# w_sp transposed by the DMA crossbar from DRAM to SBUF in place of TensorE transposes and VectorE copies, and GELU in four instructions in place of one

## The chip, the cores and the metric

The kernel runs on one core of one Trainium2 chip. The metric is the device time of one execution in microseconds (us). Before the change the median of three runs is 1141.48 us (1138.74 to 1142.0).

## What is computed

One transformer block in bfloat16 on a sequence of T = 2048 tokens of width D = 1024: a segmented attention (32 heads of 32, four segments of 512 tokens, with a memory carried from segment to segment) and, behind it, a gated MLP that mixes tokens (gMLP). The change is in the second half. Cut to what matters there:

```python
def _B_ref(x, w_in, w_sp, b_sp, w_out):            # x: layernorm of h, [1, 2048, 1024]
    Fh = w_in.shape[-1] // 2                        # 1792
    z = gelu_tanh(x @ w_in)                         # [1, 2048, 3584]
    z1 = z[..., :Fh]
    z2 = layernorm(z[..., Fh:])
    g = einsum('ts,bsf->btf', w_sp, z2) + b_sp[None, :, None]
    return (z1 * g) @ w_out
h  = x + attention(layernorm(x))
h2 = h + _B_ref(layernorm(h), w_in, w_sp, b_sp, w_out)
```

`gelu_tanh(v)` is 0.5 v (1 + tanh(0.79788 (v + 0.044715 v^3))). The sum over s with w_sp needs w_sp with s on the partitions, and w_sp lies in DRAM with t along the rows: it has to be transposed.

## The kernel before

The kernel is written instruction by instruction. `_Plan.op` (L45) appends an instruction to the list of one engine with its semaphore waits; `_Plan.dma` (L72) does it for a transfer, on the queue of SyncE (SP) or GpSimd (POOL). Each engine works its list off in the order in which the Python code appended it, so the order of the code is the order on every engine. PSUM banks are handed out in rotation by `get_misc` (L278), eight of them in the second half of the kernel.

First comes the attention (`quad`, `seg_end`, L477 and L641), which writes h to the output tensor in DRAM. Then:

- Loading and normalising h. `hn1` (L741) loads 128 tokens of h, computes the layernorm (`ln_stats`, L320: bn_stats, bn_aggr, an addition on VectorE, a power on GpSimd at L328, two more on VectorE), and `hn2` (L752) transposes the result on TensorE (L339) and copies it out of PSUM on VectorE (L760). The 16 chunks are done four for each segment of 512 tokens; those of segment s+1 are spread as extra units between the blocks of segment s.
- The w_in stage, `C1_seg` (L787), once for each of the four segments. It has 30 blocks of eight matmuls (`proj8`, L383): 14 z1 blocks (features on the partitions, 512 tokens wide) and 16 z2 blocks (128 tokens on the partitions; for each of the four groups of tokens three blocks of 512 and one of 256 features). The order is z2 group, four z1, z2 group, four z1, z2 group, three z1, z2 group, three z1. Each block is closed by one ScalarE instruction (L818), which takes GELU of the PSUM bank into `Z1T` or `Z2G` and frees the bank. After the fourth z2 block of a group `z2_ln` (L779) runs the layernorm of `Z2G` into `Z2` on VectorE and GpSimd. One extra unit (hn1 or hn2) is taken after each z2 group and after each z1 block of odd number. The weights w_in lie whole in SBUF.
- The w_sp and w_out stage, `C2C3_block` (L887), for four blocks of 512 tokens. First 14 blocks of 16 matmuls with w_sp transposed (L902), each closed by two VectorE instructions (L905 adds b_sp, L908 multiplies by z1) into `YT`; then eight blocks of 14 matmuls with w_out (L929), closed by a VectorE addition of h (L933) and a store. Before the first, SP loads b_sp (L891); before each pair of the latter, SP loads h again (L920).
- w_sp transposed, `wsp_units` (L855): for each 128 rows of w_sp one load of 512 KB into one of two buffers (`WSPCH`), 16 TensorE transposes in two banks (L876), and two VectorE copies into `WSPT[bblk % 2]` (L879). The four units of block 0 stand between the w_in stage and the first w_sp matmul; those of block b+1 are put after the 2nd, 5th, 8th and 11th of the 14 blocks of block b. The first of them and the load of w_out (on POOL's queue, L845) wait until the w_in stage is over on TensorE, VectorE and ScalarE, since their buffers lie in the memory of w_in.

Of the kernel before, what the change touches and what calls it, by code (L numbers as in the profile page):

```python
# [5 lines left out]
BF16 = mybir.dt.bfloat16  # L6
# [5 lines left out]
T = 2048  # L12
# [4 lines left out]
L = 512  # L17
# [4 lines left out]
SCALE = DH ** (-0.5)  # L22
LN_EPS = 1e-5
MEM_EPS = 1e-6
NJ = [512, 384, 256, 128]
OFFJ = [0, 512, 896, 1152]
ESLOT = 1280
# [78 lines left out]
def bass_sequential_preLN__memory_aug_infini_attn__mixer_gmlp__prompt_kernel(  # L106
# [42 lines left out]
    d_x = [mksig("d_x0", True), mksig("d_x1", True)]  # L149
    d_xr = [mksig("d_xr0", True), mksig("d_xr1", True)]  # L150
    d_hr = [mksig("d_hr0", True), mksig("d_hr1", True)]
    d_wsp = [mksig("d_wsp0", True), mksig("d_wsp1", True)]
    d_brow = [mksig("d_brow0", True), mksig("d_brow1", True)]
    d_out = [mksig("d_out0", True), mksig("d_out1", True)]

# [11 lines left out]
    def tens(name, shape, dt, off):  # L167
        sz = int(np.prod(shape[1:])) * mybir.dt.size(dt)
        assert off % 32 == 0, (name, off)
        assert off + sz <= ARENA, (name, off, sz)  # L170
        return nc.alloc_sbuf_tensor_at(name, list(shape), dt, offset=abase + off)
# [68 lines left out]
    R_CTMP = R_WQKV + 57344  # L240
    HR = [tens("hr%d" % i, [128, D], BF16, R_CTMP + i * 2048) for i in range(2)]
    HN = [tens("hn0", [128, D], BF16, R_CTMP + 4096), tens("hn1", [128, D], BF16, R_XN2)]
    R_CT2 = R_HCH + 3072
    Z2G = tens("z2g", [128, FH], BF16, R_CT2)
    WOUT = tens("w_out", [128, 14, D], BF16, R_WQKV)
    WSPT = [tens("wspT0", [128, NTC, L], BF16, R_WQKV + 28672), tens("wspT1", [128, NTC, L], BF16, R_WQKV + 45056)]
    WSPCH = [tens("wspch0", [128, T], BF16, R_WQKV + 61440), None]
    YT = tens("yT", [128, 14, L], BF16, R_WO)
    FIN2 = [tens("fin2_%d" % i, [128, L], BF16, R_WO + 14336 + i * 1024) for i in range(2)]
    TMPG = tens("tmpg", [128, L], F32, R_CT2)  # L250
    BROW = [tens("brow0", [128, L], BF16, R_CT2 + 2048)]
    HR2 = [tens("hr2_0", [128, D], BF16, R_CT2 + 3072)]
    WSPCH[1] = tens("wspch1", [128, T], BF16, R_CT2 + 5120)

    PS = nc.alloc_psum_tensor("ps", [128, 8, 512], F32)

    def bank_f32(b):
        return PS[:, b, :]
# [507 lines left out]
    def hn_chunk(tc):  # L766
        hn1(tc)
        return hn2(tc)

    z2g_res = _Res()  # L770

    hnt_ready = {}
    for (kind, tc) in (("h1", 0), ("h1", 1), ("h2", 0), ("h1", 2), ("h2", 1), ("h1", 3), ("h2", 2), ("h2", 3)):
# [3 lines left out]
            hnt_ready[tc] = hn2(tc)  # L777

    def z2_ln(tc, t4):  # L779
        t = ln_stats(Z2G, 4, LN_EPS, [t4], csz=448)  # L780
        tz = P("dve", lambda e, tc=tc: e.tensor_scalar(Z2[:, tc, :], Z2G[:], SM4[:, 1:2], SM4[:, 2:3],
                                                      ALU.mult, ALU.add),
               waits=[t], sig=g_dve_pe)
        z2g_res.free = (g_dve_pe, tz[1])
        chain["ln"] = tz

    def C1_seg(s, extra_units):  # L787
        sbk = s % 2
        xu = list(extra_units)
        wready = [hnt_ready[4 * s + i] for i in range(4)] + [_w16(t_win)]  # L790
        z1blocks = []
        for fc in range(14):
            z1blocks.append(dict(kind="z1", fc=fc, ncols=512,
                                 lhs=(lambda i, fc=fc: WIN_LO[:, i, fc * 128:(fc + 1) * 128]),
                                 rhs=(lambda i: HNT[sbk][:, i, :]),
                                 out=Z1T[:, fc, s * 512:(s + 1) * 512], accum=None))
        z2blocks = []
        for tcl in range(4):
            tc = 4 * s + tcl
            grp = []  # L800
            for fb in range(4):
                w = 512 if fb < 3 else 256
                f0 = fb * 512
                grp.append(dict(kind="z2", tc=tc, tcl=tcl, fb=fb, ncols=w,
                                lhs=(lambda i, tcl=tcl: HNT[sbk][:, i, tcl * 128:(tcl + 1) * 128]),
                                rhs=(lambda i, f0=f0, w=w: WIN_HI[:, i, f0:f0 + w]),
                                out=Z2G[:, fb * 512:fb * 512 + w], accum=None))
            z2blocks.append(grp)
        blocks = z2blocks[0] + z1blocks[0:4] + z2blocks[1] + z1blocks[4:8] + z2blocks[2] + z1blocks[8:11] + \
            z2blocks[3] + z1blocks[11:14]  # L810
        for n, blk in enumerate(blocks):
            mb = get_misc()
            ncols = blk["ncols"]
            dst = bank_f32(mb)[:, 0:ncols]
            w = [misc[mb].free] + (wready if n == 0 else [])
            tp = proj8(blk["lhs"], blk["rhs"], dst, w, g_pe_act)
            wz = [z2g_res.free] if (blk["kind"] == "z2" and blk["fb"] == 0) else []
            t4 = P("act", (lambda e, dst=dst, o=blk["out"]: e.activation(o, dst, ACTF.Gelu_apprx_tanh)),  # L818
                   waits=[tp] + wz, sig=g_act_dve)
            misc[mb].free = t4  # L820
            if blk["kind"] == "z2" and blk["fb"] == 3:
                z2_ln(blk["tc"], t4)
                if xu:
                    xu.pop(0)()
            if blk["kind"] == "z1" and blk["fc"] % 2 == 1 and xu:
                xu.pop(0)()
        while xu:
            xu.pop(0)()
# [20 lines left out]
    yt_res = _Res()  # L849
    fin_res = [_Res(), _Res()]  # L850

    wsp_ctr = [0]
    wspch_res = [_Res(), _Res()]

    def wsp_units(bblk, first_waits):  # L855
        wb = WSPT[bblk % 2]
        wspt_res[bblk % 2].ready = []

        def unit(tcl):
            tc = 4 * bblk + tcl  # L860
            k = wsp_ctr[0] % 2
            wsp_ctr[0] += 1
            ch = WSPCH[k]
            tl = plan.dma("sp", ch[:], B_w_sp[tc * 128:(tc + 1) * 128, :], d_wsp[k],
                          waits=[wspch_res[k].free] + (list(first_waits) if tcl == 0 else []))
            for half in range(2):
                mb = get_misc()
                bb = bank_bf16(mb)
                w = [misc[mb].free, _w16(tl)]
                if tcl == 0 and half == 0:  # L870
                    w.append(wspt_res[bblk % 2].free)
                    w += list(first_waits)
                tok = None
                for kk in range(8):
                    sc = half * 8 + kk
                    tok = P("pe", (lambda e, kk=kk, sc=sc, bb=bb, ch=ch: e.transpose(  # L876
                        bb[:, kk * 128:(kk + 1) * 128], ch[:, sc * 128:(sc + 1) * 128], IDENT[:])),
                            waits=(w if kk == 0 else []), sig=(g_pe_dve if kk == 7 else None))
                te = P("dve", (lambda e, half=half, bb=bb, tcl=tcl: e.tensor_copy(  # L879
                    wb[:, half * 8:(half + 1) * 8, tcl * 128:(tcl + 1) * 128],  # L880
                    bb.rearrange("p (c n) -> p c n", c=8))), waits=[tok], sig=g_dve_pe)
                misc[mb].free = te
                wspt_res[bblk % 2].ready.append(te)
            wspch_res[k].free = (g_pe_dve, tok[1])
        return [lambda tcl=tcl: unit(tcl) for tcl in range(4)]

    def C2C3_block(bblk, extra_units):  # L887
# [29 lines left out]
        for tcl in range(4):  # L917
            tc = 4 * bblk + tcl
            b = 0
            thr = plan.dma("sp", HR2[b][:], out2d[tc * 128:(tc + 1) * 128, :], d_hr[b],  # L920
                           waits=[hr_res[b].free, t_pe_all_C1, t_dve_all_C1, t_act_all_C1])
            ftoks = []
            for half in range(2):
                mb = get_misc()
                dst = bank_f32(MISC[mb])
                w = [misc[mb].free, ylast, _w16(t_wout)]
                tok = None
                for fc in range(14):
                    tok = P("pe", (lambda e, fc=fc, half=half, tcl=tcl, dst=dst: e.matmul(  # L929
                        dst, YT[:, fc, tcl * 128:(tcl + 1) * 128], WOUT[:, fc, half * 512:(half + 1) * 512],  # L930
                        start=(fc == 0), stop=(fc == 13))),
                            waits=(w if fc == 0 else []), sig=(g_pe_dve if fc == 13 else None))
                tf = P("dve", (lambda e, half=half, dst=dst, b=b: e.tensor_tensor(  # L933
                    FIN2[half][:], dst, HR2[b][:, half * 512:(half + 1) * 512], ALU.add)),
                       waits=[tok, _w16(thr), fin_res[half].free], sig=g_dve_sp)
                misc[mb].free = tf
                ftoks.append(tf)
                to = plan.dma("sp", out2d[tc * 128:(tc + 1) * 128, half * 512:(half + 1) * 512], FIN2[half][:],
                              d_out[half], waits=[tf])
                fin_res[half].free = _w16(to)  # L940
            hr_res[b].free = ftoks[-1]
# [71 lines left out]
```

The softmax here doesn't subtract the row's maximum and nothing guards it: scores larger than these inputs give would overflow.

## Time and profile before

| what | value |
|---|---|
| median of three runs | 1141.48 us |
| the profiled execution's own time | 1142.0 us |
| its span (first to last instruction) | 1140.2 us |
| mean granted TensorE clock | 0.904 of full speed |
| TensorE matmuls busy | 947.2 us (83% of the span) |
| VectorE busy | 527.8 us (46%) |
| ScalarE busy | 304.3 us (27%) |
| GpSimd busy | 35.2 us (3%) |
| data moved by DMA | 54.53 MB, 48 GB/s in the mean |

All times in the profile are microseconds from the start of the span unless ns is said. L12 is line 12 of the kernel. PE is TensorE's matmuls (a transpose is one too), PEld its weight loads, DVE VectorE, ACT ScalarE, POOL GpSimd, SP SyncE. A row of the groups reads: line, engine, operation, output <- input, shapes, count, then busy us and mean ns of one, then the engine's idle time just before such instructions and what ended it. A row of the timeline reads: start, length, engine, line, operation, count, and in brackets idle time before it and what ended that. Matmuls are pipelined and their lengths are modelled, so what counts for them is the distance from start to start.

The stages by the timeline: the w_in stage runs from 600.3 us to the end of the last GELU at 806.2; the first matmul with w_sp starts at 825.5; the last store is issued at 1138.0.

### The profile page before, as it was taken

The numbers are of one execution on the slowest core, as the hardware profiler recorded it, in microseconds if no ns is written. First come the engines' busy times: TensorE is split into PE (matmuls) and PEld (weight loads), VectorE is DVE, ScalarE is ACT, GpSimd is POOL, SyncE is SP. The second block draws the span as 40 slices with busy tenths as digits, with TensorE's granted clock in tenths as the row PEclk, the third lists the DMA queues.
The fourth block names the chain that finished last, engine by engine and source line by source line (L and its number), as shares of the span: only waits on it lengthen the run. The fifth ranks groups of instructions, "written<-read, shape, count | busy, mean of one in ns | idle before, by whom it ended". The sixth has DMA issues, their size and how long they took to land.

```text
span 1140.2 us, 16027 instructions
## 1 busy us (share of the span) xinstructions
PE 947.2 (83%) x6735; PEld 483.9 (42%) x6848; DVE 527.8 (46%) x1448; ACT 304.3 (27%) x383; POOL 35.2 (3%) x68
## 2 busy tenths in 40 slices
PE   2978886688775898566749999999599999999998
PEld 1444443444333443233324545444344444444443
DVE  4066333886447853366454553632344253343332
ACT  0356651366313652144202333333100000000000
POOL 2000000000000000000000000100000000000000
PEclk9988989798985999765678999999799999999999
DMA  8010002000020004400021000000610310301102
GB/s 324 26 29 1 1 1 83 29 1 1 1 93 20 1 1 163 169 1 1 19 92 29 19 19 19 20 1 1 238 53 1 92 61 13 112 29 37 42 1 65
DMA packets 23305, 54.53 MB, mean 48 GB/s; under 512 B 2369, under 2 KB 6977, under 8 KB 23233
## 3 DMA queue, kind: packets, MB, share of 16 engines
q1 hardware_dynamic: 19152, 34.10, 9.6%
q0 software_dynamic: 4080, 19.40, 4.5%
q8 instruction: 54, 0.88, 0.3%
q14 instruction: 19, 0.15, 0.0%
HBM read 45.10 MB, written 8.39 MB: 47 GB/s over the span
## 4 chain that ended last, share of the span: by engine, by line
PE 68%; DVE 15%; ACT 6%; DMA 4%; issue 4%; POOL 1%; SPq 0%; DVEq 0%; ACTq 0%; POOLq 0%
PE ps L386 33%; PE ps L902 17%; PE ps L929 8%; ACT eall L520 4%; PE ps L513 3%; DVE stats L323 3%; PE ps L506 2%; DMA wqkv<-in_A_wv_dram 2%; PE ps L551 2%; PE ps L876 1%; DVE ta L579 1%; DVE tm L581 1%; POOL sm_58 L328 1%; PE ps L556 1%; PE ps L339 1%
## 5 line engine op out<-in xcount | busy, mean ns | idle before, releaser
L520 ACT ACTIVATE eall<-ps 128x2048 bf16<-128x2048 f32 (+3 forms) x128 | 158.6, 1239 | 173.0 <-PE ps L513 172.4
L386 PE MATMUL ps<-xnT,wqkv 128*128 128x512 bf16 x489 | 118.6, 388 | 11.3 <-DVE msum L635 4.6
L929 PE MATMUL ps<-w_out,yT 128*128 128x512 bf16 x437 | 96.8, 379 | 6.9 <-DVE yT L908 6.4
L902 PE MATMUL ps<-wspT_113,z_106 128*128 128x512 bf16 x439 | 99.1, 386 | 1.7 <-DVE wspT_113 L879 1.3
L902 PE MATMUL ps<-wspT_114,z_106 128*128 128x512 bf16 x440 | 96.6, 379 | 0.4
L905 DVE TENSOR_TENSOR tmpg<-ps,brow_120 128x512 f32<-128x512 f32 x56 | 38.7, 692 | 118.4 <-PE ps L902 103.6
L386 PE MATMUL ps<-wo,oT 128*128 128x512 bf16 x248 | 63.9, 412 | 21.8 <-DVE oT L652 21.6
L323 DVE BATCH_NORM_STATS2 stats<-z2g 128x6 f32<-128x448 bf16 x64 | 35.3, 614 | 90.9 <-ACT z2g L818 90.9
L386 PEld LDWEIGHTS ps<-xnT,wqkv 128*128 128x128 bf16 x512 | 47.3, 99 | 62.4 <-DVE msum L635 5.8
L929 PEld LDWEIGHTS ps<-w_out,yT 128*128 128x128 bf16 x448 | 43.5, 98 | 60.2 <-DVE yT L908 8.2
L902 PEld LDWEIGHTS ps<-wspT_113,z_106 128*128 128x128 bf16 x448 | 44.0, 99 | 53.9 <-issue 3.6
L902 PEld LDWEIGHTS ps<-wspT_114,z_106 128*128 128x128 bf16 x448 | 43.7, 98 | 51.9
L818 ACT ACTIVATE z2g<-ps 128x512 bf16<-128x512 f32 x64 | 34.8, 544 | 111.4 <-PE ps L386 111.4
L386 PE MATMUL ps<-wqkv,xnT 128*128 128x512 bf16 x248 | 59.0, 391 | 4.5 <-DVE msum L635 3.6
L513 PE MATMUL ps<-negtri,ident 128*128 128x128 bf16 x512 | 61.6, 256 | 0.0
L506 PE MATMUL ps<-qT_70,kT_72 32*128 32x512 bf16 (+3 forms) x256 | 25.0, 380 | 33.6 <-ACT eall L520 33.6
L386 PE MATMUL ps<-w_in_hi,hnT_103 128*128 128x512 bf16 (+1 forms) x251 | 51.6, 364 | 1.4 <-DVE hnT_103 L760 1.2
L818 ACT ACTIVATE z1T<-ps 128x512 bf16<-128x512 f32 x56 | 33.4, 597 | 70.7 <-PE ps L386 70.7
L386 PE MATMUL ps<-hnT_104,w_in_lo 128*128 128x512 bf16 x217 | 49.4, 379 | 0.4
L386 PE MATMUL ps<-w_in_hi,hnT_104 128*128 128x512 bf16 (+1 forms) x253 | 49.6, 352 | 0.2
L386 PE MATMUL ps<-hnT_103,w_in_lo 128*128 128x512 bf16 x218 | 49.3, 379 | 0.3
L386 PEld LDWEIGHTS ps<-wo,oT 128*128 128x128 bf16 x256 | 25.6, 104 | 55.2 <-issue 13.4
(138 smaller groups left out, 1073.5 us busy)
## 6 DMA issues: line engine op xcount, KB each, us to landing
wspch_115<-in_B_w_sp_dram SPq DMA_DIRECT2D x8, 512.0 KB, 4.1
wspch_122<-in_B_w_sp_dram SPq DMA_DIRECT2D x8, 512.0 KB, 4.2
hr_0_121<-out_dram SPq DMA_DIRECT2D x16, 256.0 KB, 2.8
w_in_lo<-in_B_w_in_dram POOLq DMA_DIRECT2D x1, 3584.0 KB, 12.2
w_in_hi<-in_B_w_in_dram POOLq DMA_DIRECT2D x1, 3584.0 KB, 22.8
w_out<-in_B_w_out_dram POOLq DMA_DIRECT2D x1, 3584.0 KB, 17.8
xch_87<-in_A_x_dram SPq DMA_DIRECT2D x8, 256.0 KB, 2.8
xch_88<-in_A_x_dram SPq DMA_DIRECT2D x8, 256.0 KB, 3.0
```

The lines of the kernel that those rows point to most:

```text
L323: t = P("dve", (lambda e, ci=ci: e.bn_stats(STATS[:, ci, :], eng_in_ap[:, ci * csz:(ci + 1) * csz])), waits=((list(first_wait) + [chain["l ...
L328: tp = P("pool", lambda e: e.tensor_tensor(SM4[:, 1:2], SM4[:, 0:1], MHALF[:], ALU.pow), waits=[t], sig=g_pool)
L339: tok = P("pe", (lambda e, i=i: e.transpose(bb[:, i * 128:(i + 1) * 128], src_tile[:, col0 + i * 128: col0 + (i + 1) * 128], IDENT[:])), w ...
L386: tok = P("pe", (lambda e, i=i: e.matmul(dst, lhs_of_i(i), rhs_of_i(i), start=(i == 0), stop=(i == 7))), waits=(waits if i == 0 else []), ...
L506: P("pe", (lambda e, i=i, dst=dst: e.matmul(dst, kT[32 * i:32 * (i + 1), c, j * 128:(j + 1) * 128], qT[32 * i:32 * (i + 1), c, 128 * j:512 ...
L513: tp = P("pe", (lambda e, dstd=dstd: e.matmul(dstd, IDENT[:], NEGTRI[:], start=False, stop=True)), sig=(g_pe_act if i == 3 else None))
L520: ta = P("act", (lambda e: e.activation(dst4, src4, ACTF.Exp, scale=float(SCALE))), waits=wa, sig=g_act_pe)
L551: fn = (lambda e, i=i, j=j, h=h: e.matmul(dstb[:, i * 128:i * 128 + 33], ESALL[:, i, OFFJ[j] + (cq - j) * 128: OFFJ[j] + (cq - j + 1) * 12 ...
L818: t4 = P("act", (lambda e, dst=dst, o=blk["out"]: e.activation(o, dst, ACTF.Gelu_apprx_tanh)), waits=[tp] + wz, sig=g_act_dve)
L902: tok = P("pe", (lambda e, sc=sc, fc=fc, dst=dst: e.matmul(dst, Z2[:, sc, fc * 128:(fc + 1) * 128], wb[:, sc, :], start=(sc == 0), stop=(s ...
L905: t1 = P("dve", lambda e, dst=dst: e.tensor_tensor(TMPG[:], dst, BROW[0][:], ALU.add), waits=[tok, _w16(tb), tmpg_res.free], sig=g_dve_pe)
L929: tok = P("pe", (lambda e, fc=fc, half=half, tcl=tcl, dst=dst: e.matmul(dst, YT[:, fc, tcl * 128:(tcl + 1) * 128], WOUT[:, fc, half * 512: ...
```

## The change

Two things are done.

GELU of the w_in product, one ScalarE instruction before, is computed by four: ScalarE squares the PSUM bank (t1, Square) into `X2T`; VectorE forms (v^2 + 1/0.044715) v (t2, scalar_tensor_tensor, which reads the bank again) into `WG`; ScalarE takes Tanh of that, scaled (t3), into `TH`; VectorE forms (tanh + 1) v (t4, scalar_tensor_tensor, which reads the bank a third time and frees it) into `Z1T` or `Z2G`. t3 and t4 of a block are put after t1 and t2 of that block and ahead of t1 and t2 of the next one. The three small buffers are double. The result is twice GELU: the factor 2 falls out of the layernorm of z2 (whose eps is multiplied by 4), and for z1 it is taken out by a factor 0.5 in the last addition (L933 becomes scalar_tensor_tensor).

w_sp goes from DRAM to `WSPT` by one DMA with transposition for each 128 rows, on SP's queue, straight into the place that the VectorE copies wrote; the chunk buffers, the TensorE transposes and the copies are dropped. Each of the eight places (two buffers of four) has its own semaphore, and the w_sp matmuls wait for those of their block.

```diff
-            t4 = P("act", (lambda e, dst=dst, o=blk["out"]: e.activation(o, dst, ACTF.Gelu_apprx_tanh)),
-                   waits=[tp] + wz, sig=g_act_dve)
-            misc[mb].free = t4
...
+        for n in range(len(blocks) + 1):
+            blk = blocks[n] if n < len(blocks) else None
+            if prev is not None:
...
+                t3 = P("act", (lambda e, g=g, ncols=ncols: e.activation(TH[g][:, 0:ncols], WG[g][:, 0:ncols], ACTF.Tanh,
+                                                                    scale=float(GELU_C))),
+                       waits=[prev["t2"], th_res[g].free], sig=g_act_dve)
+                wg_res[g].free = t3
+                if prev["accum"] is None:
+                    t4 = P("dve", (lambda e, g=g, ncols=ncols, dst=dst, o=prev["out"]: e.scalar_tensor_tensor(
+                        o, TH[g][:, 0:ncols], 1.0, dst, ALU.add, ALU.mult)), waits=[t3], sig=g_dve_pe)
...
+                th_res[g].free = t4
+                misc[prev["mb"]].free = t4
+                if prev["kind"] == "z2" and prev["fb"] == 3:
+                    z2_ln(prev["tc"], t4)
+                    if xu:
+                        xu.pop(0)()
+            if blk is not None:
...
+                tp = proj8(blk["lhs"], blk["rhs"], dst, w, g_pe_act)
...
+                t1 = P("act", (lambda e, g=g, ncols=ncols, dst=dst: e.activation(X2T[g][:, 0:ncols], dst, ACTF.Square)),
+                       waits=[tp, x2t_res[g].free], sig=g_act_dve)
+                t2 = P("dve", (lambda e, g=g, ncols=ncols, dst=dst: e.scalar_tensor_tensor(
+                    WG[g][:, 0:ncols], X2T[g][:, 0:ncols], float(GELU_K), dst, ALU.add, ALU.mult)),
+                       waits=[t1, wg_res[g].free], sig=g_dve_act)
+                x2t_res[g].free = t2
+                blk["t2"] = t2
+            prev = blk
+            if blk is not None and blk["kind"] == "z1" and blk["fc"] % 2 == 1 and xu:
                 xu.pop(0)()
...
         def unit(tcl):
             tc = 4 * bblk + tcl
-            k = wsp_ctr[0] % 2
...
-            tl = plan.dma("sp", ch[:], B_w_sp[tc * 128:(tc + 1) * 128, :], d_wsp[k],
-                          waits=[wspch_res[k].free] + (list(first_waits) if tcl == 0 else []))
-            for half in range(2):
...
-                for kk in range(8):
-                    sc = half * 8 + kk
-                    tok = P("pe", (lambda e, kk=kk, sc=sc, bb=bb, ch=ch: e.transpose(
-                        bb[:, kk * 128:(kk + 1) * 128], ch[:, sc * 128:(sc + 1) * 128], IDENT[:])),
-                            waits=(w if kk == 0 else []), sig=(g_pe_dve if kk == 7 else None))
-                te = P("dve", (lambda e, half=half, bb=bb, tcl=tcl: e.tensor_copy(
-                    wb[:, half * 8:(half + 1) * 8, tcl * 128:(tcl + 1) * 128],
-                    bb.rearrange("p (c n) -> p c n", c=8))), waits=[tok], sig=g_dve_pe)
...
+            wfree = [wspt_res[bblk % 2].free] + list(first_waits) if tcl == 0 else []
+            tl = plan.dma("sp", wb[:, :, tcl * 128:(tcl + 1) * 128], B_w_sp[tc * 128:(tc + 1) * 128, :],
+                          d_wsp[4 * (bblk % 2) + tcl], waits=wfree, transpose=True)
+            wspt_res[bblk % 2].ready.append(_w16(tl))
...
-                tf = P("dve", (lambda e, half=half, dst=dst, b=b: e.tensor_tensor(
-                    FIN2[half][:], dst, HR2[b][:, half * 512:(half + 1) * 512], ALU.add)),
+                tf = P("dve", (lambda e, half=half, dst=dst, b=b: e.scalar_tensor_tensor(
+                    FIN2[half][:], dst, 0.5, HR2[b][:, half * 512:(half + 1) * 512],
+                    ALU.mult, ALU.add)),
```

Not shown: the constants `GELU_C` and `GELU_K`, the declarations of the buffers and semaphores, and 4 x eps in `z2_ln` (L780).

More of the change, by code (lines that the diff above doesn't have):

```diff
@@ L24 @@
 MEM_EPS = 1e-6
+GELU_C = 0.7978845608028654 * 0.044715
+GELU_K = 1.0 / 0.044715
 NJ = [512, 384, 256, 128]
@@ L151, in bass_sequential_preLN__memory_aug_infini_attn__mixer_gmlp__prompt_kernel @@
     d_hr = [mksig("d_hr0", True), mksig("d_hr1", True)]
-    d_wsp = [mksig("d_wsp0", True), mksig("d_wsp1", True)]
+    d_wsp = [mksig("d_wsp%d" % i, True) for i in range(8)]
     d_brow = [mksig("d_brow0", True), mksig("d_brow1", True)]
@@ L242, in bass_sequential_preLN__memory_aug_infini_attn__mixer_gmlp__prompt_kernel @@
     HN = [tens("hn0", [128, D], BF16, R_CTMP + 4096), tens("hn1", [128, D], BF16, R_XN2)]
+    X2T = [tens("x2t%d" % i, [128, L], BF16, R_CTMP + 6144 + i * 1024) for i in range(2)]
     R_CT2 = R_HCH + 3072
     Z2G = tens("z2g", [128, FH], BF16, R_CT2)
+    WG = [tens("wg%d" % i, [128, L], BF16, R_CT2 + 3584 + i * 1024) for i in range(2)]
+    TH = [tens("th%d" % i, [128, L], BF16, R_CT2 + 5632 + i * 1024) for i in range(2)]
     WOUT = tens("w_out", [128, 14, D], BF16, R_WQKV)
     WSPT = [tens("wspT0", [128, NTC, L], BF16, R_WQKV + 28672), tens("wspT1", [128, NTC, L], BF16, R_WQKV + 45056)]
-    WSPCH = [tens("wspch0", [128, T], BF16, R_WQKV + 61440), None]
     YT = tens("yT", [128, 14, L], BF16, R_WO)
@@ L252, in bass_sequential_preLN__memory_aug_infini_attn__mixer_gmlp__prompt_kernel @@
     HR2 = [tens("hr2_0", [128, D], BF16, R_CT2 + 3072)]
-    WSPCH[1] = tens("wspch1", [128, T], BF16, R_CT2 + 5120)
     PS = nc.alloc_psum_tensor("ps", [128, 8, 512], F32)
@@ L768, in hn_chunk @@
         return hn2(tc)
+    x2t_res = [_Res(), _Res()]
+    wg_res = [_Res(), _Res()]
+    th_res = [_Res(), _Res()]
     z2g_res = _Res()
+    gctr = [0]
+    t_z1_done = {}
     hnt_ready = {}
@@ L779, in z2_ln @@
     def z2_ln(tc, t4):
-        t = ln_stats(Z2G, 4, LN_EPS, [t4], csz=448)
+        t = ln_stats(Z2G, 4, 4.0 * LN_EPS, [t4], csz=448)
         tz = P("dve", lambda e, tc=tc: e.tensor_scalar(Z2[:, tc, :], Z2G[:], SM4[:, 1:2], SM4[:, 2:3],
@@ L810, in C1_seg @@
             z2blocks[3] + z1blocks[11:14]
[L811 to L818, printed above, removed]
-                   waits=[tp] + wz, sig=g_act_dve)
-            misc[mb].free = t4
[L821 to L825, printed above, removed]
+        prev = None
@@ new lines, in C1_seg @@
+        for n in range(len(blocks) + 1):
+            blk = blocks[n] if n < len(blocks) else None
+            if prev is not None:
+                g = prev["g"]
+                ncols = prev["ncols"]
+                dst = prev["dst"]
+                t3 = P("act", (lambda e, g=g, ncols=ncols: e.activation(TH[g][:, 0:ncols], WG[g][:, 0:ncols], ACTF.Tanh,
[5 more added lines that the diff above has]
+                        o, TH[g][:, 0:ncols], 1.0, dst, ALU.add, ALU.mult)), waits=[t3], sig=g_dve_pe)
+                else:
+                    t4 = P("dve", (lambda e, g=g, ncols=ncols, dst=dst, o=prev["out"], ac=prev["accum"]:
+                                  e.scalar_tensor_tensor(o, TH[g][:, 0:ncols], 1.0, dst, ALU.add, ALU.mult,
+                                                         accum_out=ac)), waits=[t3], sig=g_dve_pe)
+                th_res[g].free = t4
[5 more added lines that the diff above has]
+            if blk is not None:
+                g = gctr[0] % 2
+                gctr[0] += 1
+                blk["g"] = g
+                mb = get_misc()
+                blk["mb"] = mb
+                ncols = blk["ncols"]
+                dst = bank_f32(mb)[:, 0:ncols]
+                blk["dst"] = dst
+                w = [misc[mb].free] + (wready if n == 0 else [])
+                if blk["kind"] == "z2" and blk["fb"] == 0:
+                    w.append(z2g_res.free)
+                tp = proj8(blk["lhs"], blk["rhs"], dst, w, g_pe_act)
+                if blk["kind"] == "z1" and blk["fc"] == 13:
+                    t_z1_done[s] = tp
+                t1 = P("act", (lambda e, g=g, ncols=ncols, dst=dst: e.activation(X2T[g][:, 0:ncols], dst, ACTF.Square)),
[7 more added lines that the diff above has]
+            if blk is not None and blk["kind"] == "z1" and blk["fc"] % 2 == 1 and xu:
@@ L850, in bass_sequential_preLN__memory_aug_infini_attn__mixer_gmlp__prompt_kernel @@
     fin_res = [_Res(), _Res()]
-    wsp_ctr = [0]
-    wspch_res = [_Res(), _Res()]
     def wsp_units(bblk, first_waits):
@@ L860, in unit @@
             tc = 4 * bblk + tcl
-            k = wsp_ctr[0] % 2
-            wsp_ctr[0] += 1
-            ch = WSPCH[k]
-            tl = plan.dma("sp", ch[:], B_w_sp[tc * 128:(tc + 1) * 128, :], d_wsp[k],
-                          waits=[wspch_res[k].free] + (list(first_waits) if tcl == 0 else []))
-            for half in range(2):
[L867 to L873, printed above, removed]
-                for kk in range(8):
-                    sc = half * 8 + kk
-                    tok = P("pe", (lambda e, kk=kk, sc=sc, bb=bb, ch=ch: e.transpose(
-                        bb[:, kk * 128:(kk + 1) * 128], ch[:, sc * 128:(sc + 1) * 128], IDENT[:])),
-                            waits=(w if kk == 0 else []), sig=(g_pe_dve if kk == 7 else None))
-                te = P("dve", (lambda e, half=half, bb=bb, tcl=tcl: e.tensor_copy(
-                    wb[:, half * 8:(half + 1) * 8, tcl * 128:(tcl + 1) * 128],
-                    bb.rearrange("p (c n) -> p c n", c=8))), waits=[tok], sig=g_dve_pe)
-                misc[mb].free = te
-                wspt_res[bblk % 2].ready.append(te)
-            wspch_res[k].free = (g_pe_dve, tok[1])
+            wfree = [wspt_res[bblk % 2].free] + list(first_waits) if tcl == 0 else []
+            tl = plan.dma("sp", wb[:, :, tcl * 128:(tcl + 1) * 128], B_w_sp[tc * 128:(tc + 1) * 128, :],
+                          d_wsp[4 * (bblk % 2) + tcl], waits=wfree, transpose=True)
+            wspt_res[bblk % 2].ready.append(_w16(tl))
         return [lambda tcl=tcl: unit(tcl) for tcl in range(4)]
```

## The prediction

> **What bounds the kernel now.** I read the table of engines first (TensorE is busy 83% of the span, VectorE 46%, ScalarE 27%), then the chain that ended last, then the stages by time windows, and last the timeline of the stages that the change touches. The page's chain, in shares of the span:
>
> ```profile
> PE 68%; DVE 15%; ACT 6%; DMA 4%; issue 4%; POOL 1%; SPq 0%; DVEq 0%; ACTq 0%; POOLq 0%
> ```
>
> TensorE sets the end, but the share is a mean. The windows show the stages (columns: stretch, its length, busy us and count of PE, PEld, DVE, ACT, POOL, granted clock, DMA share, GB/s):
>
> ```profile
> 653.83:705.50 51.67, 50.28 (x269) 25.28 (x273) 25.84 (x60) 17.06 (x30) 4.40 (x8) 1.00 0.08 21
> 806.20:825.50 19.30, 7.31 (x64) 6.68 (x66) 5.54 (x8) 0.00 (x0) 1.12 (x1) 0.69 0.94 337
> 825.50:880.00 54.50, 54.19 (x283) 25.88 (x286) 22.85 (x35) 0.00 (x0) 0.00 (x0) 0.95 0.10 33
> ```
>
> The reader is to see three things. In the w_in stage (600.3 to 806.2 us; the first line is one of its four segments) TensorE is full at full clock, and GELU on ScalarE takes a third of the time, hidden. Between 806.2 and 825.5 TensorE is nearly idle and the DMA engines are 94% busy at 337 GB/s: first w_sp chunks and w_out together. In the w_sp stage (from 825.5) TensorE is full again.
>
> One block in the w_in stage, from the timeline (start, length, engine, line):
>
> ```profile
> 657.70 0.60 ACT L818 ACTIVATE z2g<-ps 128x512 bf16<-128x512 f32 x1 [1.13 <-PE ps L386]
> 659.42 0.60 ACT L818 ACTIVATE z2g<-ps 128x512 bf16<-128x512 f32 x1 [1.13 <-PE ps L386]
> 660.30 0.38 ACT L818 ACTIVATE z2g<-ps 128x256 bf16<-128x256 f32 x1 [0.28 <-PE ps L386]
> 660.71 2.21 DVE L323 BATCH_NORM_STATS2 stats<-z2g 128x6 f32<-128x448 bf16 x4 [6.94 <-ACT z2g L818]
> 662.96 0.26 DVE L325 BATCH_NORM_AGGREGATE mv<-stats 128x2 f32<-128x24 f32 x1
> 664.07 0.16 DVE L330 SCALAR_TENSOR_TENSOR sm_58<-mv,sm_58 128x1 f32<-128x1 f32 x1 [0.66 <-POOL sm_58 L328]
> 664.26 0.75 DVE L781 TENSOR_SCALAR z_106<-z2g,sm_58 128x1792 bf16<-128x1792 bf16 x1
> ```
>
> A 512-column block comes every 1.72 us (657.70 to 659.42), TensorE's eight matmuls. After each group of four z2 blocks VectorE runs a layernorm of 4.30 us (660.71 to 665.01), 0.66 of it waiting for GpSimd.
>
> **What the Trainium skill says.** "TensorE: Matmul & The Clock Gate", Architectural detail, says that ScalarE's and VectorE's queues are strict FIFO; the trace agrees (L330 and L781 wait behind GpSimd's 0.55 us step, and nothing of VectorE passes them). "ScalarE: Activation LUTs", Table sets, puts tanh in exp's set and says that cheap functions are filler in all sets; the trace has two table loads of 1283 ns in all and nothing on Square. "DMA: Bandwidth & Descriptors", Latency and other measured facts, has 261 GB/s for DMA transposes with a non-contiguous middle dimension; "VectorE: DVE Perf Modes", The three transpose paths, has 1309 ns for one 128x128 crossbar transpose. No row of the trace before shows a DMA transpose.
>
> **Part 1: GELU, of which the diff makes four instructions.** For each of 120 blocks the one L818 ACTIVATE (hidden) goes; Square and Tanh on ScalarE and two scalar_tensor_tensor on VectorE come. In program order ScalarE does tanh(n), square(n+1); VectorE does t4(n), then the layernorm if n ends a z2 group, then t2(n+1). tanh(n) needs t2(n), t4(n) needs tanh(n), and t2(n+1) stands behind t4(n). So t2, tanh, t4 of one block are in series with those of the next; two buffers do not loosen this. Prices:
>
> ```profile
> L406 DVE SCALAR_TENSOR_TENSOR pqT_74<-qe,pqT_74 128x512 bf16<-128x512 bf16 x16 | 11.1, 692 | 0.5
> L579 DVE TENSOR_TENSOR ta<-ps,rd 128x128 f32<-128x128 f32 x96 | 28.0, 291 | 3.3
> L302 ACT ACTIVATE g_53<-betab 128x32 f32<-128x32 bf16 x1 | 0.2, 229 | 1.8 <-DMA betab<-in_A_beta_dram 1.8
> 143.02 1.02 ACT L441 ACTIVATE tmpe<-ps 128x1024 bf16<-128x1024 bf16 x1 [0.31 <-DVE pk_66 L445]
> 144.07 0.69 DVE L442 TENSOR_SCALAR pk_66<-ps 128x1024 bf16<-128x1024 bf16 x1 [1.15 <-ACT tmpe L441]
> ```
>
> - t2 and t4 at 512 columns: 0.69 each (L406; L933, out of PSUM, has 692 too). At 256: between 291 at 128 and 692 at 512, 0.425.
> - tanh out of SBUF: L302 has 229 ns at 32 columns; L818's 384 and 597 ns at 256 and 512 give 0.833 ns a column; so 0.63 at 512 and 0.42 at 256, estimates.
> - hand-overs: ScalarE to VectorE 0.03 to 0.04 (144.04 to 144.07); VectorE to ScalarE 0.09 (L445 ended at 142.93, L441 began at 143.02).
> - a VectorE instruction whose data are there starts 0.08 before the end of the one ahead (four L323 of 0.61 take 2.21), so t4 to t2 is 0.61. square(n+1), 0.60, lies beside t4(n) and ends first.
>
> Period of a 512 block: 0.69 + 0.09 + 0.63 + 0.04 + 0.61 = 2.05 us against TensorE's 1.72. Of a 256 block: 0.425 + 0.09 + 0.42 + 0.04 + 0.345 = 1.32. Layernorm is no longer hidden: VectorE cannot start t2 before it ends. Sum:
> - 56 z1 blocks x 2.05 = 114.8.
> - 16 z2 groups x (3 x 2.05 + 1.32 + 4.30 + 0.03) = 188.8.
> - input layernorms of the next segment, 12 at 3.2 (two of them start at 613.64 and 616.87) and 12 copies of 0.66 (L760): 46. Where a unit stands after an odd z1 block, it fills the 0.75 in which VectorE waits for tanh; of 24 units 15 do, 9 of them copies of 0.66 and 6 of them layernorms worth 0.75: 10 off, 36 left.
>
> Together 339.6. The first GELU starts at 603.5 and its Square is over at 604.1, so the stage ends at 943.7 instead of 806.2: **+137.5**. TensorE, with eight banks to run ahead in, is off the path here. Of VectorE's own work in this stage nothing disappears. ScalarE has 240 x 0.6 = 144 us, not a bound. For bounds: if the tanh waits were covered entirely, VectorE alone would take 339.6 - 105 x 0.75 = 261, +59; if every hand-over and every wait were 0.1 us worse, 120 x 0.2 = +24 more.
>
> **Part 2: w_sp by the crossbar.** Removed in the w_sp stage: 12 chunks x 16 transposes, 1.06 us each time:
>
> ```profile
> 845.98 1.06 PE L876 MATMUL ps<-ident,wspch_122 128*128 128x128 bf16 x16
> ```
>
> TensorE is the bound there, so 12 x 1.06 = **-12.7**. The VectorE copies L879 (24 x 0.69) were hidden behind TensorE: nothing. Their replacement, SP's transposes for blocks 1 to 3, has a whole block (some 74 us) for 2.1 MB; cover is gone only below 2.1 MB / 74 us = 28 GB/s. They stand on SP's queue ahead of the hr load of L920, and block 0's ahead of the L891 load of b_sp; TensorE has eight PSUM banks for that delay (8 x 3.45 = 27 us of L902 work for b_sp, 8 x 3.02 = 24 of L929 work for hr); a load later than that would cost what goes beyond.
>
> The gap of 19.3 us before the first L902 matmul: four transposes of 512 KB instead of loads, transposes and copies, beside w_out (3.67 MB) on the same engines. From below: 2.1 MB and an equal share of w_out at the 337 GB/s of the window, 4.2/337 = 12.5, plus about 2 to land (a 256 KB load lands in 2.6): 14.5. At the page's 261 GB/s: 16 + 2 = 18. From above: 64 tiles x 1309 ns in series, 84. I take 20, slightly over the page's rate because the destination here is written in 256-byte pieces: **+0.7**, with -5 to +65 as ends.
>
> **Part 3: one-answer edits.** L933 becomes scalar_tensor_tensor: 692 ns before (L933) and after (L406), nothing. 4 x eps: nothing. A tanh table load is at most 1.3 us, in place of GELU's at 554.5: nothing.
>
> **Sum**, against the profiled execution's 1142.0 us (span 1140.2): 1142.0 + 137.5 - 12.7 + 0.7 = 1267.5. The median of three runs is 1141.48, 0.5 lower: 1267. Its own range, with hand-overs and the gap from 14.5 to 30: 1248 to 1292.
>
> **Rivals.**
> - A slow crossbar: at 84 us for four chunks the gap is +65, and each block of 74 us waits some 9 to 10 us more for its successor's chunks: +28 over three. 1267 + 65 + 28 = 1360. For it: the tile price, and that nothing before shows the operation. Against: the 261 GB/s. Half-way prices give 1300 to 1340. 25%.
> - TensorE falls to half clock in the layernorm pauses and becomes the bound: at the stage's start eight weight loads stand 0.43 apart instead of 0.21, so 104 x 3.42 + 16 x 1.71 = 383 instead of 339.6: 1310. Against: a pause lasts 4 to 8 us and eight full banks absorb a slow block or two. 5%.
> - Square and Tanh in different table sets: 240 loads x 1.283 = +308: 1575. Against: the page's filler rule. 3%.
> - Not slower: VectorE is overlapped after all. If t2 of the next block could pass t4 and the layernorm's wait, the stage would be bound by busy time alone; with some 100 us of present VectorE work and the 206 + 12.7 that may be spent, it decides at (218 - 100) / 240 = 0.49 us for each added instruction. At the cheapest pass of VectorE here (L746, 546 ns for 1024 columns; L781, 746 for 1792; so 0.41 for 512) the time would be 1142.0 - 12.7 + 0.7 = 1130. Against: 692 ns in every row with a second tensor operand, and the queue's order. 2%.
> - The chain runs shorter than worked out, by tanh waits that fall beside more of VectorE's work than I count: 1215 to 1248. 5%.
>
> The forecast has the remaining 60%. About 0.3% (3.4 us) is what a measurement of this kernel can tell from no change; slower has 0.98, faster and same 0.01 each. The range 1240 to 1350 takes in the forecast's own range, the upper part of the short chain, half clock and the half-way crossbar, leaving out about 2 in 10.
>
> **What would show it.** Right: C1 blocks spaced 2.05 us, VectorE idle 0.75 per block until tanh, TensorE idle for VectorE t4, the stage some 340 us; no L876; a gap of 15 to 25 us before L902. Wrong: Square rows with table loads between them; C1 matmuls 0.43 apart throughout; transposes landing later than 25 us, or L902 waiting for DMA in blocks 1 to 3.

## The result, and the profile after

| | before | changed |
|---|---|---|
| median | 1140.81 us (4 runs, 1138.74 to 1142.0) | 1258.99 us (4 runs, 1257.72 to 1260.2) |
| profiled execution: own time, span | 1142.0, 1140.2 us | 1259.37, 1257.6 us |
| ratio, 95% interval | | 1.1038 (1.1017 to 1.1059) |

The changed kernel is 118 us slower; 1267 was forecast. The two spans differ by 117.4 us, and the timelines say where:

| stretch | before | changed | difference |
|---|---|---|---|
| start to the first w_in matmul | 600.29 | 599.33 | -0.96 |
| w_in stage, to the end of the last GELU | 205.89 | 334.24 | +128.35 |
| gap to the first w_sp matmul | 19.32 | 21.99 | +2.67 |
| w_sp and w_out stage, to the end | 314.70 | 302.04 | -12.66 |

The chain of the changed kernel's page, in shares of the span:

```profile
PE 47%; DVE 30%; ACT 11%; issue 4%; DMA 3%; POOL 2%; SPq 2%; DVEq 0%; ACTq 0%; POOLq 0%
```

TensorE's share of the chain went from 68 to 47%, VectorE's from 15 to 30: the bound moved. Two windows of the changed kernel (length, busy us and count of PE, PEld, DVE, ACT, POOL, clock, DMA share, GB/s), the first inside the w_in stage, the second the gap:

```profile
640.00:692.00 52.00, 37.49 (x162) 17.05 (x167) 37.69 (x71) 20.48 (x39) 2.20 (x4) 0.82 0.04 11
933.63:955.50 21.87, 0.00 (x0) 0.00 (x0) 0.00 (x0) 0.00 (x0) 1.12 (x1) 0.50 0.97 268
```

In 52 us TensorE runs 162 recorded matmuls where it ran some 270 before, with VectorE at 72%. The gap is still full of DMA, at 268 GB/s where it was 337. VectorE and ScalarE in the w_in stage, from the timeline (start, length, engine, line; in brackets idle time ahead and what ended it; TensorE's rows are left out):

```profile
628.77 0.68 DVE L859 SCALAR_TENSOR_TENSOR wg_114<-x2t_111,ps 128x512 bf16<-128x512 bf16 x1
629.49 0.63 ACT L825 ACTIVATE th_116<-wg_114 128x512 bf16<-128x512 bf16 x1 [0.86 <-DVE wg_114 L859]
630.02 0.58 ACT L857 ACTIVATE x2t_112<-ps 128x512 bf16<-128x512 f32 x1
630.15 0.69 DVE L830 SCALAR_TENSOR_TENSOR z2g<-th_116,ps 128x512 bf16<-128x512 bf16 x1 [0.70 <-ACT th_116 L825]
630.75 0.68 DVE L859 SCALAR_TENSOR_TENSOR wg_115<-x2t_112,ps 128x512 bf16<-128x512 bf16 x1
...
635.61 0.42 DVE L830 SCALAR_TENSOR_TENSOR z2g<-th_117,ps 128x256 bf16<-128x256 bf16 x1 [0.48 <-ACT th_117 L825]
636.06 2.21 DVE L325 BATCH_NORM_STATS2 stats<-z2g 128x6 f32<-128x448 bf16 x4
```

This is the chain of the forecast: t2 (L859), tanh (L825), t4 (L830), then the next t2, from 628.77 to 630.75 = 1.98 us a block. VectorE waits 0.70 us for tanh, Square (L857) lies beside t4, and the layernorm (L325) starts as soon as t4 of the group's last block is over. Over the stage VectorE waits for tanh 105 times, 69.6 us in all (who waited for whom: us in total, times, longest):

```profile
DVE z2g L830 <- ACT th_116 L825: 21.4, 32, 0.7
DVE z2g L830 <- ACT th_117 L825: 19.7, 32, 0.7
DVE z1T L830 <- ACT th_116 L825: 19.5, 28, 0.7
DVE z1T L830 <- ACT th_117 L825: 9.0, 13, 0.7
```

### The profile page after: what moved, and what is told of

Its sections match the earlier page's. It is cut to its first block, busy times and chain, and to the rows that moved or that the text cites. A ratio compares the mean times of both kernels' runs of the same rounds, so it can differ in the third digit from the quotient of the medians.

```text
span 1257.6 us, 15928 instructions
## 1 busy us (share of the span) xinstructions
PE 960.5 (76%) x6480; PEld 473.2 (38%) x6592; DVE 652.9 (52%) x1656; ACT 362.0 (29%) x502; POOL 35.2 (3%) x68
## 2 busy tenths in 40 slices
DMA packets 54282, 54.53 MB, mean 43 GB/s; under 512 B 35392, under 2 KB 40000, under 8 KB 54208
## 3 DMA queue, kind: packets, MB, share of 16 engines
HBM read 36.71 MB, written 8.39 MB: 36 GB/s over the span
## 4 chain that ended last, share of the span: by engine, by line
PE 47%; DVE 30%; ACT 11%; issue 4%; DMA 3%; POOL 2%; SPq 2%; DVEq 0%; ACTq 0%; POOLq 0%
PE ps L388 16%; PE ps L920 15%; PE ps L947 8%; DVE stats L325 5%; ACT eall L522 4%; DVE z2g L830 3%; DVE z1T L830 3%; ACT th_116 L825 3%; DVE wg_114 L859 3%; DVE wg_115 L859 3%; PE ps L515 3%; ACT th_117 L825 3%; PE ps L508 2%; POOL sm_58 L330 2%; DMA wqkv<-in_A_wv_dram 2%
## 5 line engine op out<-in xcount | busy, mean ns | idle before, releaser
L388 PE MATMUL ps<-xnT,wqkv 128*128 128x512 bf16 x489 | 117.4, 385 | 10.9 <-DVE msum L637 4.6
L388 PE MATMUL ps<-w_in_hi,hnT_104 128*128 128x512 bf16 (+1 forms) x253 | 61.3, 407 | 38.0 <-DVE z_106 L788 37.8
L388 PE MATMUL ps<-w_in_hi,hnT_103 128*128 128x512 bf16 (+1 forms) x251 | 64.4, 424 | 30.2 <-DVE z_106 L788 28.4
L388 PE MATMUL ps<-wo,oT 128*128 128x512 bf16 x248 | 64.5, 415 | 21.8 <-DVE oT L654 21.4
L825 ACT ACTIVATE th_116<-wg_114 128x512 bf16<-128x512 bf16 (+1 forms) x60 | 36.9, 615 | 135.0 <-DVE wg_114 L859 135.0
L388 PEld LDWEIGHTS ps<-w_in_hi,hnT_104 128*128 128x128 bf16 x256 | 27.4, 109 | 73.4 <-DVE z_106 L788 41.3
L388 PE MATMUL ps<-hnT_103,w_in_lo 128*128 128x512 bf16 x218 | 52.2, 395 | 3.2 <-DVE z2g L830 3.0
L825 ACT ACTIVATE th_117<-wg_115 128x512 bf16<-128x512 bf16 (+1 forms) x60 | 35.2, 587 | 67.4 <-DVE wg_115 L859 67.4
L388 PEld LDWEIGHTS ps<-w_in_hi,hnT_103 128*128 128x128 bf16 x256 | 28.6, 114 | 67.4 <-DVE z_106 L788 31.2
L388 PE MATMUL ps<-hnT_104,w_in_lo 128*128 128x512 bf16 x217 | 51.0, 388 | 1.6 <-DVE z2g L830 1.3
L574 DVE TENSOR_SCALAR ps<-ps 128x4 f32<-128x4 f32 x96 | 16.2, 168 | 67.7 <-PE ps L553 64.7
```

The costliest lines, as they stand in the source:

```text
L388: tok = P("pe", (lambda e, i=i: e.matmul(dst, lhs_of_i(i), rhs_of_i(i), start=(i == 0), stop=(i == 7))), waits=(waits if i == 0 else []), ...
L825: t3 = P("act", (lambda e, g=g, ncols=ncols: e.activation(TH[g][:, 0:ncols], WG[g][:, 0:ncols], ACTF.Tanh, scale=float(GELU_C))), waits=[p ...
```

## The experiments

All medians below are beside the kernel before on the same chip, 1140.1 to 1140.5 us, and the ratios are to it. The kernels ran on three chips, so two experiments that are set against each other may also differ by the chip.

**Each part alone.** `x1_crossbar_only` is the kernel before with the w_sp part of the diff; `g1_gelu_only` is the changed kernel with that part taken back.

```diff
# x1_crossbar_only, in the kernel before
-            tl = plan.dma("sp", ch[:], B_w_sp[tc * 128:(tc + 1) * 128, :], d_wsp[k],
...
+            tl = plan.dma("sp", wb[:, :, tcl * 128:(tcl + 1) * 128], B_w_sp[tc * 128:(tc + 1) * 128, :],
+                          d_wsp[4 * (bblk % 2) + tcl], waits=wfree, transpose=True)
# g1_gelu_only: the same lines the other way round, in the changed kernel
```

> The kernel before with the crossbar part alone; GELU stays one ScalarE instruction. Theory (GELU's four instructions cost all, the crossbar gains a little): the gap between the w_in stage and the first w_sp matmul is 22 us as in the changed kernel (19.3 before), and 12 x 1.06 us of TensorE transposes are gone, so 1140.8 - 12.7 + 2.7 = 1131 us. Rival (the crossbar part costs, by transposes on SP's queue in the w_sp stage): 1141 or more.

Measured: 1131.94 us, ratio 0.9924 (0.9893 to 0.9955); gap 21.8 us.

> The changed kernel with TensorE transposes and copies put back; GELU stays four instructions. Theory: the w_in stage takes 334 us as in the changed kernel, the rest is as before, so 1140.8 + 128.4 = 1269 us. Rival (part of the loss is the crossbar's): below 1259 us.

Measured: 1268.36 us, ratio 1.1125 (1.1088 to 1.1163); w_in stage 334.3 us, gap 19.6.

The parts add up: -8.4 and +128.0 give +119.6, and the whole measured +118. GELU carries all of the loss; the crossbar part is a small gain, under 1.1% at the interval's end.

**Is it the series t2, tanh, t4?** `r1_next_before_last` runs the same instructions and moves two blocks of code.

```diff
         for n in range(len(blocks) + 1):
             blk = blocks[n] if n < len(blocks) else None
-            if prev is not None:
-                ...                       # t3, t4, layernorm of the block before
             if blk is not None:
                 ...                       # matmuls, t1, t2 of this block
+            if prev is not None:
+                ...                       # t3, t4, layernorm of the block before
             prev = blk
```

> The changed kernel with one change of order: Square and the first VectorE instruction of a block (t1, t2) are put ahead of Tanh and the second (t3, t4, and the layernorm) of the block before it. The same instructions run. Theory (t2, tanh and t4 are in series because t2 of the next block stands behind t4): VectorE no longer waits for tanh, some 105 waits of 0.70 us go, the w_in stage falls from 334 to 255 to 265 us, bound by VectorE's busy time, and the kernel takes 1180 to 1190 us. Rival (TensorE's banks, its clock or its wait for the layernorm sets the stage): 1240 us or more.

Measured: 1202.88 us, ratio 1.0552 (1.0517 to 1.0586); w_in stage 278.8 us. The sign and most of the size hold: 56 us go with the order alone. But the kernel ends 13 us above the upper end of the forecast. Its timeline shows the gain (first two rows) and where the rest is lost (last two):

```profile
640.95 0.68 DVE L838 SCALAR_TENSOR_TENSOR wg<-x2t,ps 128x512 bf16<-128x512 bf16 x1
641.54 0.68 DVE L852 SCALAR_TENSOR_TENSOR z1T<-th,ps 128x512 bf16<-128x512 bf16 x1
...
655.17 9.09 PE L388 MATMUL ps<-w_in_hi,hnT 128*128 128x512 bf16 x32 [5.57 <-DVE z L788]
...
662.33 0.69 DVE L838 SCALAR_TENSOR_TENSOR wg<-x2t,ps 128x512 bf16<-128x512 bf16 x1 [1.63 <-ACT x2t L836]
```

t2 and t4 now follow each other without a wait, 0.59 apart. But TensorE idled 5.57 us for the layernorm (L788) ahead of a z2 group, and afterwards VectorE waits 1.63 us for Square, which waits for TensorE's matmuls. Over the stage the two waits are 31.1 and 26.5 us. The diff had put the wait for the layernorm of the group before on the first matmul of the next group; the kernel before had it on the instruction that writes `Z2G`. My prediction did not mention this moved wait. Two kernels test it.

```diff
-                if blk["kind"] == "z2" and blk["fb"] == 0:
-                    w.append(z2g_res.free)
+                blk["wz"] = [z2g_res.free] if (blk["kind"] == "z2" and blk["fb"] == 0) else []
...
-                        o, TH[g][:, 0:ncols], 1.0, dst, ALU.add, ALU.mult)), waits=[t3], sig=g_dve_pe)
+                        o, TH[g][:, 0:ncols], 1.0, dst, ALU.add, ALU.mult)), waits=[t3] + prev["wz"], sig=g_dve_pe)
```

> The changed kernel; only the wait for the layernorm of the z2 group before, which the diff put on the first matmul of a z2 group, is moved to the VectorE instruction that writes the buffer (t4). Theory (the chain t2, tanh, t4 of VectorE and ScalarE is the bound, TensorE has slack for that wait): no change, 1259 us, though TensorE's 66 us of idling for the layernorm go or turn into waits for a bank. Rival (TensorE's wait for the layernorm is a part of the loss): 1190 to 1245 us.

Measured, in the changed kernel: 1259.55 us, ratio 1.1023 (1.0997 to 1.1048); w_in stage 334.7 us. No change. The longest of TensorE's waits in the w_in stage, of the changed kernel and then of this one:

```profile
PE ps L388 <- DVE z_106 L788: 66.3, 12, 6.5
```

```profile
PE ps L388 <- DVE z1T L830: 46.8, 12, 6.4
```

The 66 us of TensorE waiting for the layernorm (L788) are a large number without a price: taken away, TensorE waits for t4 (L830) to free a bank instead, and longer for the input layernorm (27.4 us where it was 16.3), and the end does not move.

> The changed kernel with t1, t2 ahead of the t3, t4 of the block before, and with the wait for the layernorm moved from the matmul to t4. Theory (once VectorE's tanh waits are gone, TensorE's wait for the layernorm, 31 us in the reordered kernel, and VectorE's 27 us of waiting for Square behind it are what kept the stage at some 278 us): the stage comes to VectorE's busy time, 255 to 260 us, and the kernel takes 1180 to 1186 us. Rival (those waits are covered): 1200 us or more.

Measured, both edits: 1180.81 us, ratio 1.0348 (1.0326 to 1.0371); w_in stage 258.5 us. With the order changed as well, the same moved wait is worth 22 us (20 in the stage). VectorE's waits in this stage are down to those for GpSimd's power and a few for Square:

```profile
DVE sm L332 <- POOL sm L330: 18.5, 28, 0.7
DVE wg L837 <- ACT x2t L835: 7.9, 6, 4.3
```

VectorE is busy 227.4 us of the stage's 258.5, waits 26.4 us in these two rows, and spends the last 5 in short gaps. So of the 128 us that GELU costs, 76 (334.2 to 258.5) are order and waits that the two edits take away. Of the 53 that stay (258.5 - 205.9), 22 are VectorE's busy time beyond the length of the old stage (227.4 - 205.9), and 31 are waits and gaps that this kernel still has. The wait for GpSimd's power was there before too, 18.5 us, but then hidden behind TensorE.

**The layernorm in series.** The same cut in both kernels; the four bn_stats, bn_aggr, addition, power and shift of z2's layernorm are left out.

```diff
-        t = ln_stats(Z2G, 4, 4.0 * LN_EPS, [t4], csz=448)
+        t = t4
```

> The changed kernel without the statistics of the layernorm of z2: Z2G is scaled and shifted by whatever scalars lie there, so the output is not the reference's. Theory (the layernorm is in series with the blocks): each of 16 groups is shorter by the statistics, 2.21 + 0.26 + 0.15 + 0.66 + 0.16 and their gaps = 3.6 us, so 1259 - 57 = 1202 us. Rival (the layernorm is hidden as before the change, behind TensorE or tanh): 1255 us or more.

Measured: 1203.26 us, ratio 1.0545 (1.0521 to 1.0569); w_in stage 277.2 us, 57.1 less.

> The kernel before without the statistics of the layernorm of z2 (the same cut as in the changed kernel; the output is not the reference's). Theory (before the change the layernorm is hidden behind TensorE's matmuls): no change, 1138 to 1141 us. Rival (it was on the path already, so that its 57 us are no part of the change's cost): 1085 to 1120 us.

Measured: 1135.67 us, ratio 0.9961 (0.9948 to 0.9974). A small miss: the kernel before gains 4.4 us. In its w_in stage TensorE waits 3.4 us for the input layernorm (L746), which stands behind z2's layernorm on VectorE:

```profile
PE ps L339 <- DVE hn_109 L746: 3.4, 3, 1.1
```

With the statistics gone that row is gone too, and the stage is 3.8 us shorter. So the same instructions were worth 4 us before and are worth 57 after.

**What sets the gap.** In the changed kernel SP's queue shows the transposes themselves (start, length for all four):

```profile
933.63 18.91 SPq L91 DMA_TRANSPOSE wspT_119<-in_B_w_sp_dram  x4
934.13 1.12 POOL L91 DMA_DIRECT2D w_out<-in_B_w_out_dram  x1 [7.47 <-DVE z1T L830]
953.40 9.98 SPq L91 DMA_TRANSPOSE wspT_120<-in_B_w_sp_dram  x4
```

The first four hold SP 4.7 us each in the mean, the next four 2.5. The mean hides that the first four are not alike: one by one they take 2.09, 10.63, 4.09 and 1.96 us, and the long one is issued 1.6 us after w_out's load. `w1_crossbar_wout_late` is the crossbar part alone with w_out's load behind the first four:

```diff
+    t_wout = plan.dma("pool", WOUT[:], B_w_out.rearrange("(c p) n -> p c n", p=128), d_wout,
+                      waits=fw0 + list(wspt_res[0].ready))
```

> The crossbar part alone, with the load of w_out put behind the landing of the first four w_sp transposes. Theory A (the first four transposes take 4.7 us each because w_out shares the DMA engines): they take 2.5 us each as the next four do, the gap falls from 22 to about 12.5 us, and the kernel takes about 1131 - 9.5 = 1121.5 us. Theory B (SP's own work of issuing sets 4.7 us): the gap stays 22 us, 1131 us.

Measured: 1122.43 us, ratio 0.9846 (0.9815 to 0.9878); gap 12.9 us. Its queue:

```profile
804.36 10.46 SPq L89 DMA_TRANSPOSE wspT<-in_B_w_sp_dram  x4
815.50 20.96 SPq L89 DMA_TRANSPOSE wspT<-in_B_w_sp_dram  x4
817.49 1.12 POOL L89 DMA_DIRECT2D w_out<-in_B_w_out_dram  x1 [15.25 <-DMA wspT<-in_B_w_sp_dram]
```

The slow four are now the second four, those beside w_out, again with one long one among them (11.09 us). So it is w_out's load beside them, not SP's own work of issuing. The two do not share equally: in the 10 us from 938 of the changed kernel w_out's queue moved 820 packets of 4096 bytes, 3.36 MB, and SP's queue 569 of 256 bytes, 0.15 MB. The transposes nearly stand still until w_out has landed. By packets the two are much nearer to each other than by bytes; why w_out wins is not tested here.

`d1_transposes_twice` doubles the twelve later transposes:

```diff
+            if bblk >= 1:
+                dum_tok[0] = plan.dma("sp", DUM[:], B_w_sp[tc * 128:(tc + 1) * 128, :], d_dum,
+                                      waits=[_w16(dum_tok[0])] + list(fw0), transpose=True)
```

> The crossbar part alone, with each of the twelve transposes of blocks 1 to 3 issued twice: first into a place that nothing reads, and for that one after the landing of the one before. Theory (a block of 74 us covers four transposes of about 5 us from issue to landing twice over): no change against the crossbar part alone, 1130 to 1134 us. Rival (transposes beside the w_sp matmuls cost, by SP's queue or by SBUF): 1138 us or more.

Measured: 1129.7 us, ratio 0.9912 (0.9889 to 0.9935), against 0.9924 for the crossbar part alone. The cover holds twice over.

`f1_crossbar_early` puts the first four beside matmuls:

```diff
+        if s == NSEG - 1:
+            blocks = z2blocks[0] + z1blocks[0:2] + z2blocks[1] + z1blocks[2:4] + z2blocks[2] + z1blocks[4:6] + \
+                z2blocks[3] + z1blocks[6:14]
...
-    for u in wsp_units(0, fw0):
+    for u in wsp_units(0, [t_hi_done[0]]):     # the last matmul that reads WIN_HI
```

> The crossbar part alone with w_out's load behind the first four transposes; besides, in the last segment the four z2 groups are put two z1 blocks apart so that eight z1 blocks come last, and the first four transposes wait only for the last matmul that reads the high half of w_in, whose memory they write. Theory (the gap is the four transposes, 10.5 us of issue and 2 to land, which 8 x 1.72 = 13.8 us of matmuls can cover): the gap falls from about 13 to 1 to 2 us, and the kernel takes about 1122.4 - 11.5 = 1111 us. Rival (transposes beside matmuls are slower, or slow TensorE's reads): 1117 us or more.

Measured: 1102.82 us, ratio 0.9667 (0.9643 to 0.9691), the fastest here and faster than both kernels. The gap is gone: the first w_sp matmul (L886) starts right behind the last w_in matmul.

```profile
789.28 13.98 PE L386 MATMUL ps<-hnT,w_in_lo 128*128 128x512 bf16 x64
789.48 9.49 SPq L89 DMA_TRANSPOSE wspT<-in_B_w_sp_dram  x4
803.10 27.14 PE L886 MATMUL ps<-wspT,z 128*128 128x512 bf16 x125
```

Against `w1_crossbar_wout_late` the spans differ by 16.0 us: 13.7 of gap, 2.0 in the w_sp and w_out stage, and 0.4 ahead of the gap, where kernels with the same code differ by as much or more. I had counted 11.5: the gap closed wholly, and the w_sp stage no longer begins with matmuls 0.43 us apart instead of 0.21, as it does where TensorE has been idle (ten of them in `w1_crossbar_wout_late`, 2 us in all). The medians differ by more, 19.6 us: the profiled execution of this kernel took 1106.38 us, 3.6 above its median, and runs of this kernel spread over 6 us; what the medians show beyond the 16.0 is not explained. The new order of the last segment was not run alone; with it the w_in stage takes 206.3 us against 205.1, so it is no gain there by itself.

## Why the prediction was right, point by point

- **The mechanism of part 1 is shown.** t2, tanh and t4 are in series because t2 stands behind t4: reordering the same instructions takes 56 us off, and 78 with the moved wait. The layernorm's term (16 times 3.6 of the 4.3 us) measured 57 us against 57 expected. The forecast's lower bound counts 105 waits for tanh, since input layernorms and copies fill 15 of the 120; there were 105.
- **Its size was 9 us too high**: +137.5 forecast, +128.35 measured. In the whole the forecast was 8 us too high, since the gap was 2.0 larger than forecast and the stretch ahead of the w_in stage 1.0 shorter. The term of part 1 that was mis-sized is the hand-over from VectorE to ScalarE, taken as 0.09 us from one pair of rows (L445 to L441); in the changed kernel t2 ends at 629.45 and tanh starts at 629.49, 0.04. Over 120 blocks that is 6 us. Together with t2 at 0.68 and 0.60 from t4 to t2, it makes the period of a 512 block 1.98 instead of 2.05, which over 104 blocks is 7.3 of the 9.
- **tanh out of SBUF** measured 0.63 us at 512 columns and 0.42 at 256, as estimated from L302 and L818; t2 and t4 of 256 columns measured 0.41 and 0.42 against 0.425.
- **Part 2's -12.7** measured -12.66. That it agrees to the tenth is chance: the w_sp and w_out stage takes 313.8 to 314.7 us in the three kernels here with TensorE transposes and 301.5 to 303.0 in those with the crossbar, `f1_crossbar_early` apart. The cover of the later transposes stands (`d1_transposes_twice`).
- **The gap** was taken as 20 us and measured 22.0, and that it came so near is in part luck. The sum gave w_out an equal share: 4.2 MB in some 18 us, which is 233 GB/s, and 2 us to land. In the trace w_out goes through ahead of most of the transposes and the gap moves all of both, 5.9 MB (21.87 us at 268 GB/s). Two errors of opposite sign nearly cancel. The Trainium skill ("DMA: Bandwidth & Descriptors", Latency and other measured facts) gives 261 GB/s for DMA transposes with a non-contiguous middle dimension, measured on one kernel; here four of 512 KB (2.1 MB) without w_out beside them take 9.5 to 10.5 us of issue, 200 to 221 GB/s, and the measurement decides. Beside w_out they take 18.9. The Trainium skill's 1309 ns for one 128x128 tile ("VectorE: DVE Perf Modes", The three transpose paths) do not add up tile by tile: 16 tiles take about 2.5 us in a row, 0.16 each. That was the slow crossbar's price, and it is excluded.
- **Half clock** fell with `a0_ln_wait_moved`: matmuls 0.43 apart do appear after pauses (ten in 4.42 us from 640.51; at the start of the stage before, twelve weight loads from 600.29 on stand so, not eight), the granted clock is 0.82 in the window above, but the end does not depend on TensorE there: with its waits for the layernorm taken away the stage is as long as before.
- **Table sets**: the changed kernel has one table load, 1283 ns, for the whole run, one fewer than before. So Exp, Square and Tanh ran on one load. For exp and tanh the Trainium skill ("ScalarE: Activation LUTs", Table sets) led one to expect it, since it lists both in one set; for Square this run shows it.
- **The rival "not slower"** needs more than order: with the order and the wait changed the stage still takes 258.5 us, 53 above 205.9, near the lower bound in the forecast (+59). t2 and t4 took 0.68 and 0.69 us, where the break-even worked out for this rival was 0.49.
- **Missed**: the wait that the diff moved from ScalarE to TensorE. It costs nothing in the changed kernel and 22 us as soon as the order is changed. Because of it one sign of being right did not come as named: TensorE was to idle for t4, and it idles 7 us for t4 and 66.3 for the layernorm (L788).

## What to carry to other kernels

When one instruction that frees a PSUM bank becomes a ping-pong between two engines, lay out both queues in program order and add up the chain of one block: with one instruction of the next block behind the last of this one, double buffers do not help, and putting the next block's first step ahead does. Ask which work was hidden behind the old bound: the same layernorm cost 4 us before and 57 after. A big sum of waits on an engine that has slack is worth nothing until the bound moves, and then it can be the next one. A transfer's price likewise depends on what is loaded beside it, which here held one transpose for 10.6 us, and on whether other work covers it.

## What the runs showed that was not expected

- A DMA transpose of 512 KB holds SP's queue 2.0 to 3.6 us in the first four of `w1_crossbar_wout_late` and `f1_crossbar_early`, and up to 11.1 beside a 3.67 MB load, where an ordinary load of the same 512 KB holds it 0.33 to 0.45. In those first four it lands 4.7 to 5.8 us after its issue begins.
- The transposes move in small packets: those under 512 B rise from 2369 to 35392, about 32768 = 16 x 2048 rows of 256 bytes. The page's sum of HBM reads falls by 8.4 MB, just w_sp's size, though all of it is read: that sum seems to leave DMA transposes out. `d1_transposes_twice`, which moves 6.3 MB more than the crossbar part alone, has the same sum, 36.71 MB.
